# An attention and two-layer feed-forward kernel: its low parts and weight sums between GpSimd and VectorE, in a new order of the whole program

## The chip, the cores and the metric

One core of a Trainium2 chip runs the kernel. The metric is the device time of one execution in microseconds (us). PE is TensorE, DVE VectorE, ACT ScalarE, POOL GpSimd, and SP SyncE, which here issues all DMAs.

## The reference

```python
def _attn_ref(q, k, v):                      # (2, 8, 768, 64) each, float32
    k_sum = k.reshape(B, H, nb, 32, D).max(axis=3)
    v_sum = v.reshape(B, H, nb, 32, D).mean(axis=3)
    scores_l = scale * np.matmul(q, k.transpose(0, 1, 3, 2))
    mask_l = np.abs(pos[:, None] - pos[None, :]) < 16
    scores_s = scale * np.einsum('bhsd,bhnd->bhsn', q, k_sum) + np.log(32)
    a = softmax(concat([where(mask_l, scores_l, -1e9), scores_s]))
    return np.matmul(a, np.concatenate([v, v_sum], axis=2))

def _moe_ref(x, w_in, w_out):                # 1536 tokens, 512 -> 2048 -> 512
    h = x @ w_in
    return (h * np.clip(h + 3.0, 0.0, 6.0) / 6.0) @ w_out

def _moe2_ref(x, w_in, w_out):
    h = x @ w_in
    return (h / (1.0 + np.exp(-h))) @ w_out
```

The output is `_moe2_ref(_moe_ref(attention))`, with the heads side by side in the 512 columns.

## The kernel before

**Attention.** Each of the two batches has 12 windows of 64 queries. A window sees 96 neighbouring keys and 24 block maxima, so 120 columns for each pair of heads. `load` (L463) brings 256 rows of q, k or v: either by `load_pairs` (L456), two rows of 64 numbers in one piece of 512 bytes, followed by a reordering copy `by_parity` (L480, "par" in the order, one half on DVE and one on ACT); or by two DMAs in pieces of 256 bytes that land in the final order. `tr` transposes on PE (L500). `k_copy` and `k_max` (L504, L512) make the transposed keys and the block maxima. `keys u` (L586) gathers both into one tile for window u, and `scores n` (L596) multiplies them for the two windows 2n and 2n+1; it writes two banks, unit 2n for even heads and 2n+1 for odd ones. Then come `masked` (DVE, L616), `exps` (ACT, L634), `normal` (DVE or POOL, L654), `turn` (transposition on PE, L661), `turned` (its copy, L667) and `mix n` (product with the values, L672, PE rows L679). `load_v u` (L576) loads the values of window u, into one of four buffers while u is below 16, so that `load_v 4` to `load_v 7` wait for `mix 0` and `mix 1`. `mixed_hi` and `mixed_lo` (L697, L703) store the result in two parts: a rounded high part and, as the rest, a low part. `v_sums`, `v_add` and `v_rows` make the block means of v.

**Feed-forward.** Every operand is such a pair of high and low part, and each product is three matmuls (high-high, high-low, low-high). A weight half is fetched (`fetch h`, half 2f of w_in and 2f+1 of w_out), put together from its 16-bit pieces (`conv_top`, `conv_join`), and split into `conv_hi` (L443) and `conv_lo` (L448). A step is `hidden` (L711, PE, 12 matmuls in two parts), `act` (ACT), `gate` (DVE), `gate_hi` and `gate_lo` (L770, L774: the two parts of the gated values), and `project` (L803, PE rows L798 and L801). The first 24 steps go this way. The other 72 get their hidden values from seven products instead of eight (`prod` and `prodb`, PE rows L1025). These need sums and differences of weights (`ssum` L977, split by `s_hi`, `s_lo` L1006) and of tokens (`tsum`, split by `t_hi`, `t_lo` L927; `tsumb`, `t_hib`, `t_lob` L970), and DVE additions that join the products (`join` L1068, `joinb` L1056; rows L1072 and L1066).

**What sets the order.** One table, `ORDER`, names about 1,960 such operations in one sequence. The program records them in that sequence; each engine then runs its own in that order and waits by semaphores for the others. A star behind an entry puts it on DVE where the operation can go to two engines. `rouse` and `warm` are matmuls that compute nothing and keep PE running.

```python
def gate_lo(i):
    ...
    eng = nc.vector if STEPS[i][3] == WIDE or ("gate_lo", i) in ON_DVE else nc.gpsimd
```

All steps are WIDE (512 columns), so before the change every `gate_lo` is on DVE, as are all `ssum`, `s_lo`, `t_lo`, `t_lob` and `finish_lo` (L883, the low part of the first layer's output).

Of the kernel before, what the change touches and what calls it, by code (L numbers as in the profile page):

```python
# [111 lines left out]
load k 0 1, zero, table 0, rouse 0, warm 6, load k 0 2, par k 1 0, load k 0 0, par k 1 1, par k 2 1, grow 9,  # L112
par k 2 0, rouse 4, par k 0 1, tr k 0 1 0, k_copy 0 1 0*, tr k 0 1 1, load q 0 0, tr k 0 2 0, clear,
load k 1 0, par k 0 0, tr k 0 2 1, par q 0 1, k_copy 0 2 0*, rouse 5, tr k 0 0 0, fetch 0, k_max 0 2 0,
k_copy 0 0 0, par q 0 0, k_max 0 2 1, tr k 0 0 1, k_max 0 0 1, tr q 0 0 1, k_max 0 1 1, k_max 0 0 0,
k_max 0 1 0, k_copy 0 0 1, keys 1*, tr q 0 0 0, q_copy 0 0 0*, rouse 1, keys 2, k_copy 0 1 1, tr k 1 0 1,
tr k 1 0 0, k_max 1 0 1, q_copy 0 0 1, keys 3, scores 1, keys 0, k_copy 0 2 1, scores 0, keys 6, keys 4,
table 1, conv_top 0*, keys 5, rouse 3, masked 2, load q 0 1, load v 0 0, keys 7, tr q 0 1 0, exps 2, guard 2,
v_sums 0 0, q_copy 0 1 0, k_copy 1 0 1*, masked 0, exps 0, guard 0, masked 1, masked 3, inverse 2, exps 3,
tr q 0 1 1, normal 2, inverse 0, normal 0, guard 3, q_copy 0 1 1*, turn 2, turned 2, load q 0 2, load v 0 1,  # L120
load v 0 2, conv_join 0, exps 1, scores 2, rouse 2, turn 0, v_sums 0 1, grow 6, conv_hi 0*, inverse 3,
fetch 1, normal 3, turned 0*, v_add 0 0, masked 4, conv_lo 0, tr q 0 2 1, q_copy 0 2 1, k_max 1 0 0, guard 1,
inverse 1, tr q 0 2 0, exps 4, q_copy 0 2 0, v_add 0 1, v_sums 0 2, v_add 0 2, unstage, v_rows 0, scores 3,
conv_top 1*, normal 1, v_put 0 2*, turn 3, masked 6, load k 1 1, turn 1, masked 7, guard 4, v_put 0 0,
v_put 0 1, tr k 1 1 0, turned 3, v_put 0 3, conv_join 1, tr k 1 1 1, k_copy 1 1 0*, load k 1 2, exps 6,
k_copy 1 1 1, tr k 1 2 0, conv_hi 1*, masked 5, load_v 2, guard 6, inverse 6, inverse 4, load_v 0, exps 7,
k_max 1 2 0, k_max 1 1 0, keys 9, k_copy 1 0 0*, keys 11, keys 10, tr k 1 2 1, k_copy 1 2 1, scores 5,
load_v 3, load v 1 0, guard 7, normal 6, inverse 7, k_max 1 2 1, turn 6, normal 7*, mix 1, load_v 1,
k_copy 1 2 0, load q 1 0, normal 4, turn 7, masked 10, load_v 7, exps 5, masked 11, turned 1, load_v 6,
guard 5, turn 4, mix 0, turned 7*, keys 8, scores 4, turned 6*, exps 11, v_pair 1 0, guard 11, inverse 11,  # L130
inverse 5, conv_lo 1, k_max 1 1 1, load_v 4, v_sums 1 0, tr q 1 0 1, normal 5*, turned 4, normal 11, masked 8,
load_v 5, keys 12, exps 10, guard 10, tr q 1 0 0, inverse 10, q_copy 1 0 0, mixed_hi 1, turn 5, mixed_hi 0,
masked 9, turned 5, turn 11, mixed_lo 1, mix 3, normal 10, turn 10, q_copy 1 0 1*, load q 1 1, keys 13,
turned 11, mixed_hi 3*, mixed_lo 3, scores 6, fetch 2, turned 10, mixed_lo 0, keys 14, keys 15, mix 2,
scores 7, mixed_hi 2*, mixed_lo 2, tr q 1 1 1, exps 8, guard 8, exps 9, masked 14, inverse 8, tr q 1 1 0,
conv_top 2*, conv_join 2, guard 9, fetch 4, q_copy 1 1 0, hidden 0 0, q_copy 1 1 1, conv_top 4, hidden 0 1,
act 0, conv_hi 2*, inverse 9, normal 9*, normal 8, turn 8, conv_join 4, conv_hi 4*, masked 12, exps 14,
load v 1 1, conv_lo 2, load v 1 2, turned 8, exps 12, gate 0, gate_hi 0*, keys 17, guard 12, turn 9,
gate_lo 0, masked 13, hidden 1 0, hidden 1 1, turned 9, keys 16, scores 8, conv_lo 4, fetch 6, hidden 2 0,
conv_top 6, v_pair 1 1*, v_pair 1 2*, guard 14, load_v 8, exps 13, v_sums 1 1, conv_join 6, v_sums 1 2,  # L140
conv_hi 6, v_add 1 0, v_add 1 1, hidden 2 1, guard 13, inverse 12, normal 12*, v_add 1 2, act 1, masked 15,
inverse 13, normal 13*, load_v 9, grow 1, fetch 3, conv_top 3, conv_join 3, mix 4, gate 1, turn 12, turned 12,
v_rows 1, conv_hi 3*, act 2, v_put 1 0, masked 16, gate_hi 1, conv_lo 6, hidden 3 0, hidden 3 1, conv_lo 3,
gate 2, gate_hi 2*, mixed_hi 4, v_put 1 1, load_v 11, load_v 10, mix 5, gate_lo 1, mixed_lo 4, fetch 5,
conv_top 5, exps 15, mixed_hi 5, v_put 1 2, turn 13, fetch 8, conv_join 5, project 0 0, masked 17, conv_top 8,
conv_join 8, v_put 1 3, project 1 0, project 0 1, act 3, load_v 12, gate_lo 2, guard 15, conv_hi 8, keys 19,
project 1 1, conv_lo 8, fetch 7, conv_hi 5*, conv_lo 5, conv_top 7*, load_v 13, turned 13, mix 6, load q 1 2,
gate 3, inverse 14, inverse 15, mixed_hi 6*, conv_join 7, tr q 1 2 1, hidden 4 0, hidden 4 1, keys 18,
exps 17, guard 17, inverse 17, mixed_lo 6, mixed_lo 5, normal 14*, fetch 9, normal 15, conv_top 9*,
conv_join 9, exps 16, guard 16, conv_hi 7, q_copy 1 2 1, turn 15, turned 15, turn 14, turned 14*, normal 17,  # L150
turn 17, conv_lo 7, inverse 16, tr q 1 2 0, gate_hi 3, turned 17*, q_copy 1 2 0, project 2 0, normal 16*,
fetch 12, load_v 15, gate_lo 3, load_v 14, mix 7, scores 9, mixed_hi 7*, keys 20, mixed_lo 7, masked 19,
fetch 10, conv_top 10, project 3 0, turn 16, conv_join 10, act 4, conv_hi 10*, conv_lo 10*, masked 18, gate 4,
gate_hi 4*, conv_top 12, conv_join 12, exps 18, hidden 8 0, hidden 8 1, load_v 17, fetch 11, conv_hi 9,
conv_lo 9, hidden 10 0, hidden 10 1, act 8, gate 8, turned 16, act 10, project 3 1, conv_top 11, conv_join 11,
gate_hi 8*, conv_hi 11*, exps 19, guard 19, hidden 5 0, guard 18, hidden 5 1, gate_lo 4, project 4 0,
inverse 19, normal 19*, fetch 13, grow 0, conv_top 13, conv_lo 11, conv_join 13, act 5, load_v 16, turn 19,
gate 10, project 2 1, mix 8, mixed_hi 8, gate 5, fetch 14, conv_top 14*, inverse 18, conv_hi 13, gate_hi 5*,
gate_lo 5, keys 21*, turned 19*, hidden 11 0, hidden 11 1, project 5 0, act 11, normal 18, conv_hi 12*,
scores 10, conv_lo 13*, gate 11, load_v 19, fetch 18, turn 18, turned 18, conv_join 14, conv_hi 14, gate_lo 8,  # L160
load_v 18, keys 23*, masked 20, masked 21, conv_lo 12, conv_lo 14*, conv_top 18, conv_join 18, grow 5,
exps 20, project 4 1, fetch 15, hidden 6 0, conv_top 15*, keys 22, ssum 4 1, hidden 6 1, act 6, gate 6,
hidden 7 0, hidden 7 1, mix 9, gate_hi 6, gate_lo 6, tsum 0 1 1, exps 21, project 6 0, guard 21, act 7,
gate 7, hidden 12 0, hidden 12 1, load_v 21, guard 20, mixed_lo 8, inverse 20, normal 20*, conv_join 15,
conv_hi 15*, project 6 1, conv_lo 15, scores 11, fetch 16, inverse 21, act 12, normal 21*, project 5 1,
gate_hi 7, gate_lo 7, gate 12, gate_hi 12*, project 7 0, project 7 1, mixed_hi 9, turn 20, finish 0 0 0 0,
finish 0 0 0 2, masked 22, mixed_lo 9, finish 0 0 0 1, turn 21, turned 21, masked 23, exps 23, hidden 14 0,
turned 20*, hidden 14 1, act 14, conv_top 16*, gate_lo 12, project 8 0, hidden 13 0, load_v 20, hidden 13 1,
project 12 0, exps 22, guard 22, gate 14, inverse 22, normal 22, gate_hi 14, grow 2, gate_lo 14, mix 10,
load_v 22, turn 22, turned 22, guard 23, inverse 23, normal 23, project 8 1, project 12 1, turn 23,  # L170
project 14 0, grow 3, conv_join 16, grow 8, mixed_hi 10*, mixed_lo 10, ssum 4 2, turned 23, ssum 4 3, act 13,
# [1103 lines left out]
```

## Time and profile before

| | |
|---|---|
| median of 3 executions | 585.9 us (585.74 to 586.0) |
| the profiled execution | 585.98 us |
| its span, first to last instruction | 584.1 us |
| PE busy | 566.9 us, 97% of the span, granted clock 1.00 |
| DVE busy | 462.3 us, 79% |
| ACT busy | 269.6 us, 46% |
| POOL busy | 95.8 us, 16% |

The profiled execution took 1.9 us more than its span, which is the start and the end around it. A busy share is a mean: the first 50 us are attention alone, and from then on attention, feed-forward steps and weights overlap. Instructions that are pipelined overlap in the rows by some 0.1 us, and matmuls by up to 0.17 us, because their ends are modelled; so this text takes the time of a piece of work from its start to the start of the next.

### The profile page before, as it was taken

Reading aid. Unit: us, or ns where it says so; the run is one execution under the profiler, and the core shown is the slowest. Engines: PE = TensorE matmul, PEld = TensorE weight load, DVE = VectorE, ACT = ScalarE, POOL = GpSimd, SP = SyncE. Lnnn points to the kernel's source line nnn. Section 1 sums busy time; section 2 is a strip of 40 time slices with the busy share of each in tenths; the row PEclk is TensorE's granted clock in tenths of the full one; section 3 lists DMA queues with packets and bytes.
Section 4 is the critical chain, followed back from the end, with each engine's and each line's share of the span. In section 5 each row is a group of like instructions: output and inputs, shape, how many; then the busy total and the mean of one; then the engine's idle time right before and its main releaser. Section 6 shows DMA issues by size and latency. Waiting matters only on the chain.

```text
span 584.1 us, 9467 instructions
## 1 busy us (share of the span) xinstructions
PE 566.9 (97%) x3536; PEld 476.7 (82%) x3536; DVE 462.3 (79%) x1012; ACT 269.6 (46%) x626; POOL 95.8 (16%) x111
## 2 busy tenths in 40 slices
PE   6778999999999999999999999999999999999997
PEld 6667788888888788888888888888888898888886
DVE  4899888874776999998999999585877686757764
ACT  4798865542313345541646565545534234424220
POOL 1756252101010012121100202000100000111000
PEclk9999999999999999999999999999999999999999
DMA  9999982323010112333220110223122211210013
GB/s 239 258 191 261 214 202 87 100 64 98 0 38 0 51 57 73 109 89 119 80 71 3 37 37 30 79 77 125 50 73 83 98 37 36 73 66 8 1 71 146
DMA packets 69054, 51.57 MB, mean 88 GB/s; under 512 B 36368, under 2 KB 63504, under 8 KB 69008
## 3 DMA queue, kind: packets, MB, share of 16 engines
q1 hardware_dynamic: 69008, 50.97, 33.2%
q8 instruction: 28, 0.46, 0.3%
...
## 4 chain that ended last, share of the span: by engine, by line
PE 88%; DVE 5%; DMA 3%; ACT 2%; issue 1%; SPq 0%; POOL 0%; DVEq 0%
PE bank L1025 29%; PE bank L801 22%; PE bank L798 20%; PE bank L721 11%; PE bank L679 2%; PE bank L665 1%; DMA stage<-in_v_dram 1%; PE bank L608 1%; DMA early_units<-in_v_dram 1%; ACT early_units L637 1%; DVE kmax L514 1%; DMA cst<-in_consts_dram 1%; PE bank L500 1%; DVE w L928 0%; DVE bits L435 0%
## 5 line engine op out<-in xcount | busy, mean ns | idle before, releaser
L801 PE MATMUL bank<-w,g 128*128 128x512 f32 (+1 forms) x477 | 111.7, 385 | 0.0
L798 PE MATMUL bank<-g,w 128*128 128x512 f32 x444 | 108.7, 391 | 0.4 <-DVE g L778 0.4
L801 PEld LDWEIGHTS bank<-w,g 128*128 128x128 f32 x477 | 88.2, 188 | 17.7
L450 POOL TENSOR_TENSOR w<-bits,w 128x512 fp32r<-128x512 f32 x34 | 47.9, 1411 | 304.0 <-ACT w L446 213.5
L798 PEld LDWEIGHTS bank<-g,w 128*128 128x128 f32 x444 | 82.5, 188 | 17.7 <-DVE g L778 0.8
L1025 PE MATMUL bank<-w,x 128*128 128x512 f32 (+1 forms) x360 | 73.9, 348 | 0.5 <-DVE w L971 0.5
L1025 PEld LDWEIGHTS bank<-w,x 128*128 128x128 f32 x360 | 59.4, 189 | 10.0 <-DVE w L971 0.8
L1025 PE MATMUL bank<-x,w 128*128 128x512 f32 (+1 forms) x240 | 49.6, 348 | 0.0
L426 ACT CAST top<-words 128x512 f16<-128x512 bf16 x51 | 39.7, 778 | 19.9 <-DVE bits L435 11.0
L721 PE MATMUL bank<-x,w 128*128 128x512 f32 x192 | 47.7, 396 | 0.0
L435 DVE SCALAR_TENSOR_TENSOR bits<-words,top 128x512 uint32<-128x512 uint32 x47 | 35.6, 756 | 14.0 <-ACT top L426 11.8
L1025 PEld LDWEIGHTS bank<-x,w 128*128 128x128 f32 x240 | 39.1, 189 | 5.5
L721 PEld LDWEIGHTS bank<-x,w 128*128 128x128 f32 x192 | 35.3, 188 | 7.8 <-issue 0.4
L778 DVE TENSOR_TENSOR g<-values,g 128x512 fp32r<-128x512 f32 x46 | 32.6, 712 | 7.4 <-ACT g L772 7.0
L752 ACT ACTIVATE values<-values 128x512 f32<-128x512 f32 x35 | 22.0, 628 | 29.3 <-DVE values L1066 17.0
L798 PE MATMUL bank<-w,w 128*128 128x512 f32 x132 | 33.6, 392 | 0.0
L752 ACT ACTIVATE r<-r 128x512 f32<-128x512 f32 x27 | 17.0, 629 | 28.9 <-DVE r L1072 20.0
L1072 DVE TENSOR_TENSOR values<-bank,values 128x512 f32<-128x512 f32 x39 | 26.5, 687 | 3.1 <-PE bank L1025 2.6
L798 PEld LDWEIGHTS bank<-w,w 128*128 128x128 f32 x132 | 24.5, 188 | 5.1 <-issue 0.2
L450 POOL TENSOR_TENSOR w<-cst,w 128x512 fp32r<-128x512 f32 x10 | 14.2, 1418 | 87.8 <-DVE w L446 60.6
L1025 PE MATMUL bank<-w,w 128*128 128x512 f32 (+1 forms) x144 | 28.1, 337 | 0.0
L772 ACT CAST g<-values 128x512 fp32r<-128x512 f32 x33 | 20.4, 621 | 16.7 <-PE bank L801 6.5
(192 smaller groups left out, 984.8 us busy)
## 6 DMA issues: line engine op xcount, KB each, us to landing
...
```

The costliest lines, as they stand in the source:

```text
L426: copier("conv_top", h)(out=top[:, 1], in_=src[:, 2])
L435: nc.vector.scalar_tensor_tensor(out=bitss.take(h, bit_users(h)), in0=rest, scalar=13, in1=tops.use(h).bitcast(U32), op0=ALU.logical_shift ...
L450: eng.tensor_tensor(out=w_half(h, 1), in0=bitss.use(h).bitcast(F32), in1=w_half(h, 0).bitcast(F32), op=ALU.subtract,)
L679: nc.tensor.matmul(ps[D * e : D * e + D, o : o + QW], v[:NSLOT, h * D : (h + 1) * D], own(pTs, 2 * n + e)[:NSLOT, hp * P + QW * w : hp * P ...
L721: nc.tensor.matmul(ps[:, :n], w[:, a, kk * P : (kk + 1) * P], x[:, o // SUB : (o + n) // SUB, b, kk, :], start=(m == 0), stop=(m == last),)
L752: nc.scalar.activation(out=r, in_=ps, **kind)
L772: copier("gate_hi", i)(out=g[:, 0, cols], in_=value(i)[:, cols])
L778: eng.tensor_tensor(out=g[:, 1, cols], in0=r[:, cols], in1=g[:, 0, cols].bitcast(F32), op=ALU.subtract)
L798: nc.tensor.matmul(ps[:, o : o + n], lhs, g[:, b, shift : shift + n], **flags)
L801: nc.tensor.matmul(ps[:, : len(cols)], g[:, a, rows], rhs, **flags)
L1025: nc.tensor.matmul(ps, lhs(a, kk), rhs(b, kk), start=(i == 0), stop=(i == 5))
L1072: nc.vector.tensor_tensor(out=out, in0=banks.use(("prod", p, k)), in1=r, op=ALU.add)
```

## The change

Five things change.

- `gate_lo`, `ssum`, `s_lo`, `t_lo`, `t_lob` and `finish_lo` may now go to POOL. 20 of 96 `gate_lo`, 17 of 48 `ssum`, 18 of 48 `s_lo`, 11 of 16 `t_lo`, 3 of 8 `t_lob` and 4 of 10 `finish_lo` do. The other way, 14 of 44 `conv_lo`, 7 of 21 pairs of `keys` copies and 5 of 14 `normal` move from POOL to DVE.
- The first q block is loaded in two DMAs by parity, without `load_pairs` and `by_parity`.
- The first `scores` reads the keys and maxima where they lie, in 32 matmuls for 16, and `keys 0` and `keys 1` go.
- The three `v_sums` of a batch add up in one bank, and `v_add` is one copy for a copy and two additions.
- The `ORDER` table is new except for its last 463 entries, which stand in the same sequence, some on another engine; there are 12 `rouse` for 6.

```diff
+    def adder(*op):
+        return (nc.vector if op in ON_DVE else nc.gpsimd).tensor_tensor
...
-        if b == 0 and (what == "k" or T == 0):
+        if b == 0 and what == "k":
             load_pairs(parts.take((what, b, T), 2), src, b, T)
...
+        if done == 0:
+            banks.take(("v", b), 1)
+        ps = banks.see(("v", b))
...
-                    start=(r == 0),
-                    stop=(r == 1 - b),
+                    start=(done == 0 and r == 0),
+                    stop=(done == 2 and r == 1 - b),
...
+    def v_add(b):
+        nc.vector.tensor_copy(out=vsum, in_=banks.use(("v", b))[:, :P])
...
+        if n < DIRECT:
+            near = [key_rows(b)[:, :, (t + w) * QW : (t + w) * QW + LOC] for w in range(2)]
+            pieces = [(0, near), (LOC, [kmax[b]] * 2)]
+        else:
+            pieces = [(0, [own(kws, 2 * n + w) for w in range(2)])]
...
-        eng = nc.vector if STEPS[i][3] == WIDE or ("gate_lo", i) in ON_DVE else nc.gpsimd
+        eng = nc.vector if ("gate_lo", i) in ON_DVE else nc.gpsimd
...
-        nc.vector.tensor_tensor(
+        adder("t_lo", layer, a, n)(
...
-gate_hi 82*, gate_lo 77, fetch 60, project 77 0, gate_hi 78, gate_lo 78, project 77 1, gate_hi 79,
+gate_hi 82*, gate_lo 77*, fetch 60, project 77 0, gate_hi 78, gate_lo 78*, project 77 1, gate_hi 79,
```

**SP, the loads that stand ahead of the values of windows 4 and 5.** Before, from the load of the second v block (`stage` with in_v) on; `early_w` with in_k or in_q are the 256-byte loads, `words` are weights, `early_units` and `early_r` with in_v are `load_v`, and `early_w` with in_v is `load v 1 0`, the first v block of batch 1:

```order
L458 DMA stage_84<-in_v_dram 128x8x128
L458 DMA stage_80<-in_v_dram 128x8x128
L418 DMA words_70<-in_moe_w_out_dram 128x2047
L473 DMA early_w_88<-in_k_dram 128x8x64 x4
L581 DMA early_units<-in_v_dram 96x8x64
L581 DMA early_r_97<-in_v_dram 80x8x64
L581 DMA early_units<-in_v_dram 96x8x64
L458 DMA early_w_88<-in_v_dram 128x8x128
L581 DMA early_r_97<-in_v_dram 96x8x64
L473 DMA early_w_88<-in_q_dram 128x8x64 x2
L581 DMA early_units<-in_v_dram 96x8x64 x2
L581 DMA early_r_97<-in_v_dram 96x8x64 x2
```

The same stretch now, to the same last row:

```order
L478 DMA early_w_88<-in_k_dram 128x8x64 x2
L478 DMA early_w_88<-in_q_dram 128x8x64 x2
L588 DMA early_units<-in_v_dram 96x8x64
L421 DMA words_69<-in_moe_w_in_dram 128x4x511
L588 DMA early_r_97<-in_v_dram 96x8x64
L423 DMA words_70<-in_moe_w_out_dram 128x2047
L588 DMA early_units<-in_v_dram 96x8x64
L478 DMA early_w_88<-in_k_dram 128x8x64 x2
L588 DMA early_r_97<-in_v_dram 80x8x64
L478 DMA early_w_88<-in_q_dram 128x8x64 x2
L588 DMA early_units<-in_v_dram 96x8x64 x2
L588 DMA early_r_97<-in_v_dram 96x8x64 x2
```

`load v 1 0` has left this stretch; it now stands two weight halves behind its end. Every other load up to the last row stands ahead of it before and now, among themselves in another order.

**PE, the first feed-forward step.** The names are `scores` (L608), `tr` of the next q block (L500), `hidden` (L721, 12 matmuls a step) and `turn` (L665). Before, from the end of `scores 7` on:

```order
L608 MATMUL bank_72<-early_units,early_w_89 64x120 x2
L500 MATMUL bank_73<-cst,early_w_88 128x128 x4
L500 MATMUL bank_74<-cst,early_w_88 128x128 x4
L721 MATMUL bank_79<-x_0_64,w_87 128x512 x12
L665 MATMUL bank_77<-cst,early_w_95 120x128 x4
L665 MATMUL bank_74<-cst,early_w_95 120x128 x4
L721 MATMUL bank_73<-x_0_64,w_386 128x512 x12
```

Now:

```order
L680 MATMUL bank_72<-cst,early_units 120x128 x4
L680 MATMUL bank_74<-cst,early_w_95 120x128 x4
L736 MATMUL bank_78<-x_0_64,w_86 128x512 x12
L736 MATMUL bank_79<-x_0_64,w_87 128x512 x12
L623 MATMUL bank_75<-early_units,early_w_89 64x120 x2
```

`turn 9`, which stood between the first two steps, now stands ahead of both, together with one more turn, and the two steps follow each other. `scores 7`, `v_sums 1 0`, `turn 11` and both `tr q 1 1` (the two L500 rows) have gone from ahead of the first step to behind the second.

**POOL, in the middle of the program** (the first weight sums of the seven-product scheme). Before, only `conv_lo` (L450) and the last `normal` (L657) stand there:

```order
L450 TENSOR_TENSOR w_1265<-bits_67,w_1265 128x512
L657 TENSOR_TENSOR early_w_95<-early_w_95,stat_103 128x480
L657 TENSOR_TENSOR early_w_95<-early_w_95,stat_100 128x480
L450 TENSOR_TENSOR w_1594<-cst,w_1594 128x512
L450 TENSOR_TENSOR w_1594<-bits_68,w_1594 128x512
```

Now `gate_lo` (L793), `ssum` (L1009), `t_lo` (L943), `t_lob` (L986) and `s_lo` (L1023) stand among the `conv_lo` (L455):

```order
L793 TENSOR_TENSOR g_92<-values,g_92 128x512
L1009 TENSOR_TENSOR words_70<-bits_68 128x256
L1009 TENSOR_TENSOR words_70<-bits_67,bits_68 128x256
L1009 TENSOR_TENSOR words_70<-words_70,bits_67 128x256
L1009 TENSOR_TENSOR words_70<-bits_67,words_70 128x256
L793 TENSOR_TENSOR g_1719<-values,g_1719 128x512
L455 TENSOR_TENSOR w_1544<-bits_68,w_1544 128x512
L943 TENSOR_TENSOR w_491<-values,w_491 128x512
L986 TENSOR_TENSOR x_late<-r_1720,x_late 128x512
L1023 TENSOR_TENSOR x_1_65<-words_70,x_1_65 128x256 x2
```

Eleven low parts and sums that were DVE's are POOL's here, with one `conv_lo` among them.

## Rows read from the trace of the kernel before

**Rows 1.** Page: busy time, share of the span and instructions of each engine.

```profile
PE 566.9 (97%) x3536; PEld 476.7 (82%) x3536; DVE 462.3 (79%) x1012; ACT 269.6 (46%) x626; POOL 95.8 (16%) x111
```

**Rows 2.** Stage: us, busy time (instructions) of PE, PEld, DVE, ACT, POOL; clock, DMA share, GB/s.

```profile
30.00:45.00 15.00, 11.49 (x190) 9.37 (x188) 13.54 (x74) 13.92 (x57) 9.73 (x15) 1.00 1.17 192
```

**Rows 3.** Waits of PE from 51 to 575 us: total, times, longest.

```profile
PE bank L1025 <- DVE w L971: 0.5, 1, 0.5
PE bank L798 <- DVE g L778: 0.4, 1, 0.4
```

**Rows 4.** PE in order of time, 40 to 62 us: start, length, instructions, [idle before].

```profile
40.11 0.69 PE L679 MATMUL bank<-early_g,early_r 120*64 120x64 f32 x16 [0.54 <-DMA early_r<-in_v_dram]
...
47.65 1.15 PE L679 MATMUL bank<-early_g,early_r 120*64 120x64 f32 x32
48.73 1.05 PE L608 MATMUL bank<-early_units,early_w 64*64 64x120 f32 x32
49.85 1.09 PE L500 MATMUL bank<-cst,early_w 128*128 128x128 f32 x8
50.70 3.00 PE L721 MATMUL bank<-x,w 128*128 128x512 f32 x12
53.54 0.60 PE L665 MATMUL bank<-cst,early_w 128*120 128x128 f32 x4
55.35 0.62 PE L665 MATMUL bank<-cst,early_w 128*120 128x128 f32 x4 [1.21 <-DVE early_w L657]
55.73 3.01 PE L721 MATMUL bank<-x,w 128*128 128x512 f32 x12
...
59.65 1.67 PE L721 MATMUL bank<-x,w 128*128 128x512 f32 x6
61.25 0.71 PE L545 MATMUL bank<-early_w,cst 128*32 128x128 f32 x16
```

**Rows 5.** DVE in order of time, 48 to 54 us.

```profile
48.85 0.69 DVE L701 CAST x<-bank 128x512 fp32r<-128x512 f32 x1 [0.57 <-PE bank L679]
49.57 0.69 DVE L705 TENSOR_TENSOR x<-bank,x 128x512 fp32r<-128x512 f32 x1
...
53.45 1.75 DVE L657 TENSOR_TENSOR early_w<-early_w,stat 128x480 f32<-128x480 f32 x1
```

**Rows 6.** SP's issues in order of time, and the landing of the load issued at 31.78.

```profile
30.74 0.67 SPq L581 DMA_DIRECT2D early_units<-in_v_dram  x1
31.78 0.66 SPq L458 DMA_DIRECT2D early_w<-in_v_dram  x1
...
41.16 1.60 SPq L581 DMA_DIRECT2D early_r<-in_v_dram  x2
...
DMA to landing us min/median/max: 7.3/7.3/7.3
```

**Rows 7.** The landing of the load issued at 30.74.

```profile
DMA to landing us min/median/max: 6.0/6.0/6.0
```

**Rows 8.** ACT, released by the landings of the k block 0 and the first q block.

```profile
8.91 0.62 ACT L486 COPY stage<-stage 128x512 f32<-128x512 f32 x1 [1.18 <-DMA stage<-in_k_dram]
10.78 0.62 ACT L486 COPY stage<-stage 128x512 f32<-128x512 f32 x1 [1.25 <-DMA stage<-in_q_dram]
```

**Rows 9.** The landing of the next load's second half, in pieces of 256 bytes.

```profile
L473 SPq DMA_DIRECT2D early_w<-in_k_dram x1: 1736/1736/1736, 7.0 to 7.0; - x1
...
DMA to landing us min/median/max: 6.1/6.1/6.1
```

**Rows 10.** By line: one instruction in ns, min/median/max, first and last start.

```profile
L778 DVE TENSOR_TENSOR g<-values,g x46: 676/686/1776, 68.8 to 565.0; 128x512 fp32r<-128x512 f32 x46
L1072 DVE TENSOR_TENSOR values<-bank,values x39: 680/685/693, 228.7 to 557.7; 128x512 f32<-128x512 f32 x39
L450 POOL TENSOR_TENSOR w<-bits,w x34: 1274/1302/1823, 25.0 to 538.5; 128x512 fp32r<-128x512 f32 x34
```

**Rows 11.** Busy time by stage, columns as in rows 2, in the seven-product part.

```profile
200.00:225.00 25.00, 24.50 (x130) 20.84 (x129) 24.13 (x46) 8.81 (x17) 2.48 (x2) 1.00 0.16 52
```

More of the change, by code (lines that the diff above doesn't have):

```diff
@@ L111 @@
 ORDER = """
[L112 to L171, printed above, removed]
@@ new lines @@
+normal 9, mix 3, mixed_hi 3*, mix 2, scores 6, mixed_lo 0, k_copy 1 1 1, turn 10, mixed_hi 2, mixed_lo 3,
+mixed_lo 2, fetch 2, conv_top 2, exps 11, fetch 4, keys 17*, conv_join 2, conv_hi 2, turn 9, masked 13,
+hidden 0 0, hidden 0 1, k_copy 1 2 0, conv_top 4, conv_lo 2*, turned 10, keys 15, hidden 1 0, hidden 1 1,
+guard 11, keys 14, scores 7, masked 12, conv_join 4, load v 1 0, inverse 11, act 0, gate 0, v_pair 1 0*,
+grow 1, turned 9, v_sums 1 0, normal 11, turned 8*, turn 11, load q 1 1, conv_hi 4, conv_lo 4, exps 13,
@@ new lines @@
+conv_hi 10, guard 14, v_put 1 3*, conv_lo 10*, v_put 1 2, hidden 5 0, act 4, gate_hi 3, gate 4, load q 1 2,
+tr q 1 2 1, fetch 7, inverse 14, hidden 5 1, exps 16, project 2 1, gate_lo 3, mixed_lo 4, mixed_lo 5,
+normal 14*, conv_top 7*, conv_join 7, act 5, conv_hi 7, fetch 9, gate 5, q_copy 1 2 1*, keys 18*, guard 16,
+conv_lo 7*, inverse 17, turn 15, turn 14, conv_top 9*, load_v 13, load_v 12, normal 17*, load_v 15, gate_hi 5,
+mix 6, turned 14, tr q 1 2 0, grow 0, inverse 16, normal 16, conv_join 9, project 3 0, project 3 1, fetch 11,
@@ new lines @@
+project 6 0, gate_lo 7*, hidden 15 0, hidden 15 1, act 15, fetch 18, hidden 13 1, turn 19, exps 20,
+conv_lo 15, project 7 0, guard 20, masked 21, project 6 1, act 13, turned 19, exps 21, load_v 18, grow 5,
+load_v 19, project 7 1, mix 9, load_v 21, inverse 20, normal 20*, keys 23*, gate 13, gate_hi 8*,
+finish 0 0 0 0, keys 22, conv_top 19*, conv_join 19, scores 11, grow 2, guard 21, inverse 21, gate 15,
+finish 0 0 0 1, fetch 16, conv_top 18, conv_hi 19*, turn 20, turned 20, normal 21*, turn 21, turned 21,
@@ new lines @@
+finish 0 0 0 3, gate_lo 8, project 8 0, masked 23, hidden 14 0, hidden 14 1, masked 22, exps 22, exps 23,
+act 14, guard 22, load_v 20, project 9 0, finish 0 0 0 2, guard 23, mix 10, hidden 12 0, conv_lo 19,
+inverse 23, normal 23*, inverse 22, project 8 1, project 9 1, normal 22*, gate_hi 15, hidden 12 1, gate 14,
+gate_hi 10, turn 22, gate_lo 10*, mixed_hi 10, mixed_hi 9, mixed_lo 9, tsum 0 3 0, act 12, load_v 22,
+turned 22, gate 12, turn 23, conv_join 18, gate_lo 15, project 10 0, hidden 11 0, gate_hi 14, mixed_lo 10,
```

373 lines of the change are left out of this document (206 added, 167 removed).

## Prediction

> **What bounds the kernel now.** I read the page first. PE is busy for 97% of the span, DVE for 79%, POOL for 16% [rows 1]. A change that moves work between DVE and POOL can therefore only gain what PE loses by waiting, and the question is where that is. From 51 to 575 us PE waited three times for more than a moment: the two shortest [rows 3], and the one of 1.21 us at 55.35, where `turn 9` waits for `normal 9` [rows 4]. Together these are 2.1 us. The rest of the idle time lies ahead of 51 us: in 30 to 45 us PE is busy for 11.5 of 15 us, while DVE has 13.5, ACT 13.9, and the DMA share is above 1 [rows 2]. So the head of the program is held by loads and by two engines at once, and ends where the first feed-forward step starts, at 50.70 [rows 4]. From there on PE has filler work for nearly every moment.
>
> What holds that first step is a chain that the rows show link by link. `mix 0` waits for a load of values until 40.11. Its end frees the buffers for the values of windows 4 and 5, which SP issues from 41.16 [rows 6]. `mix 2`, which reads them, starts at 47.65 [rows 4]; `mixed_hi 2` starts at 48.85 and `mixed_lo 2` at 49.57 [rows 5]; PE fills in `scores 7` and two transpositions, and the step starts at 50.70. The chain's first link is the SP queue.
>
> **The head: loads.** All loads that stood ahead of `mix 0`'s last one, and of those of windows 4 and 5, stand ahead of them after the change too, except `load v 1 0`. Its price: it was issued at 31.78 and landed 7.3 later, at 39.1; the load before it was issued at 30.74 and landed 6.0 later, at 36.7 [rows 6, 7]. The queue thus gave it 2.4 us, which the chain no longer waits for. Against this, the first q block now comes in pieces of 256 bytes. In pieces of 512 it took from 8.91 to 10.78, 1.87 us [rows 8]; the k block behind it, of the same size in pieces of 256, ended at 7.0 + 6.1 = 13.1, so it took 2.3 [rows 9]. That is 0.4 more. The Trainium skill's page "DMA: Bandwidth & Descriptors", section "Specifications", asks for at least 512 bytes in a transfer for the full rate and so speaks against this edit; the trace agrees in the sign, by a quarter and not more. If the chain keeps its length of 10.6 us, the first step starts at 50.70 - 2.4 + 0.4 = 48.7.
>
> This isn't a gain of 2 us, because less has been done by then. `scores 7` (48.73 to 49.85, 1.1), two transpositions (to 50.70, 0.85), one `turn` (55.35 to 55.73, 0.4) and half of the 0.7 that two `v_sums` take now come later; two turns (0.8) come earlier [rows 4]. Net 1.9 us of PE's work is still to do, so the start that changes nothing is 50.70 - 1.9 = 48.8. The term is **-0.1**. Its bounds: if the q block costs nothing more, -0.5; if the chain isn't led by the queue but by DVE, which the next paragraph prices, +3.
>
> **The head: the other engines.** `keys 0`, `keys 1`, two reordering copies and two `v_add` on DVE and ACT go; DVE takes five `normal`, several `keys` and two `conv_lo` or so of POOL's. I count about 1.2 us more of DVE work ahead of `mixed_lo 2` than before, at 0.6 to 0.7 for an instruction of 512 columns [rows 10]. DVE had 1.5 us of 15 free [rows 2], some 4 us over 45, so it is covered if DVE's waits fall well, and costs 1.2 if not. I take nothing. The twice 16 matmuls of the first `scores` for 1.05 us [rows 4] and the six more `rouse` lie where PE has nothing else to do; if not, they cost 1 us. One copy for three `v_add`s is off the chain as well.
>
> **The wait at 55.35.** `normal 9` stood on DVE behind a POOL instruction and took 1.75 us [rows 5]; `turn 9` behind the first step waited for it. Now `turn 9` stands ahead of the first step and its `normal` is POOL's, early. The wait goes: **-1.2**. What could be late instead is the second step, which now follows the first at once; its low part of weights is DVE's, after `mixed_lo 2`, and has the 2.84 us of the first step for two casts and a subtraction. I take nothing for it, and 0.5 as its bound.
>
> **Fewer changes of kind.** From the first step on PE alternated between runs of feed-forward and attention 19 times, now 17. A run of 12 matmuls took 2.84 (50.70 to 53.54), one of six 1.60 (59.65 to 61.25), 0.18 more than half of that [rows 4]. Two runs fewer: **-0.4**, and nothing as the other bound.
>
> **The middle.** These two waits [rows 3] are for a `t_lo` and a `gate_lo` on a DVE that is busy for 24.1 of 25 us there [rows 11]. DVE hands over 38 instructions of 512 columns at 0.69, 26 us, and 35 of 256; it takes back 14 `conv_lo` and, on balance, some 15 others, at most 20 us. It has more room, and I let both waits go: **-0.9**.
>
> What POOL's side costs: a low part takes 1.30 there against 0.69, and each holds up the other engine. The DVE row of `gate_lo`, two operands in SBUF, goes from 686 up to 1776 ns; the row that reads a bank never exceeds 693; POOL's own goes from 1302 up to 1823 [rows 10]. The Trainium skill's page "SBUF — State Buffer", section "Who interferes with whom", calls this an exclusive lock of a shared port, by which the later of the two waits for the whole instruction of the other; it speaks against every move to POOL. By the rows a move costs the chain behind it at most 1.82 - 0.69 = 1.1 plus one blocked instruction of 1.1. The chain from a product to the `project` that reads it is a join, `act`, `gate` and `gate_hi` at about 0.7 each, and the low part: 4.1 to 4.6 us with POOL. In the new order at least 24 matmuls lie between, 33 where POOL makes the low part; at 2.84 / 12 = 0.24 these are 5.7 and 7.8 us. In the old order the shortest lead was some 17, 4 us, and left no wait at its place [rows 3]. I take nothing for new waits; the bound is 15 places of 0.3, +4.5.
>
> **Sum.** 585.98 - 0.1 - 1.2 - 0.4 - 0.9 = 583.4, made against the profiled execution, which is 0.1 above the median of 585.9. I forecast **583.4**, 0.4% faster. About 0.2% (1.2 us) is what a measurement of this kernel can tell from no change.
>
> **Rivals.**
> - *The head comes late by what is saved.* DVE or ACT lead the chain, and the 1.2 us of extra DVE work and its waits push the first step to 51 or so: 583.4 + 2.3 = 585.7. For it: DVE 13.5 and ACT 13.9 of 15 [rows 2]. Against: the rows at 40.11 and 47.65 show loads at the head of the chain. It's the case in which the change does nothing.
> - *One queue wait holds all of SP* (slower). `load q 1 0` needs a buffer that a transposition frees which now stands on PE behind `turn 6`, and that waits for DVE's `normal 6`. SP is in order, so the four loads of values stand behind it. If `normal 6` is 4.5 us late, the first step starts at 53.2: 583.4 + 4.5 = 587.9. From a start at 51.3 on it's no gain at all, and each us is a us. For it: the loads at 41.16 were issued only when `mix 0` had ended [rows 6], so SP does stand still in this stretch; against: nothing shows `normal 6` that late.
> - *POOL as the new wait* (slower by the same mark): the lock above, at 15 of the 73 new places for 0.3 us: 587.9. It decides from 2.6 us of new waits on. For it: POOL's instructions are 1.3 to 1.8 long; against: the leads.
> - *The head gains more*: loads run 2 us ahead of the old queue because fewer of them wait for a buffer, and the first step starts at 46.7: 581.4. DVE has too little room for more.
>
> **How the numbers follow.** Forecast 0.48, head late 0.2, queue wait 0.1, POOL 0.1, larger gain 0.12. The forecast's own range, with the bounds of the q block, the second step, the alternations and 1 us of new waits, is 582.2 to 585.0; I count 0.46 of its 0.48 as faster by over 0.2%, with the larger gain 0.58. The late head is within 0.2%, with the rest of the forecast 0.22. The two others make 0.2 slower. The range for 8 times in 10 reaches from 581.2 to 587.2.
>
> **What would show it.** The first step's start (48.7; no gain from 51.3 on), the end of `mix 0` and the last landing ahead of `mix 2`; no wait at `turn 9`; 17 runs; PE's waits from 51 to 575 us, with their releasers: none by POOL over 0.3 us if I'm right. DVE's busy time should fall by 10 to 30 us and POOL's rise by 30 to 60 with no effect on the time. The prediction is wrong if PE waits for POOL at many places, or if the first step starts at 51 or later.

## The result: 0.7% slower

The changed kernel took 589.9 us in the median of 4 runs (589.59 to 590.79) beside 585.85 us for the kernel before, a ratio of 1.0067 (95% interval 1.0056 to 1.0079). A second series gave 1.0064 (1.0049 to 1.0078). The forecast was 583.4 us, its range 581.2 to 587.2: wrong in sign, and outside the range.

The page of the profiled execution (589.95 us, span 588.2): busy time, and the busy tenths of 40 slices for DVE, POOL and PE's clock.

```profile
PE 572.0 (97%) x3592; PEld 481.1 (82%) x3592; DVE 459.8 (78%) x971; ACT 262.1 (45%) x617; POOL 151.9 (26%) x151
...
DVE  4789989766869898888989999647677687657764
...
POOL 1136313421030743222223474423310000111000
PEclk9989999999999999999999999999999999999999
```

POOL took 56 us more than in [rows 1], DVE only 2.5 less. PE's waits from 51 to 575 us, as in [rows 3] (total, times, longest):

```profile
PE bank L1040 <- DVE acc L862: 2.2, 2, 1.9
PE bank L1040 <- DVE values L1087: 0.8, 1, 0.8
PE bank L816 <- DVE r L1087: 0.6, 1, 0.6
PE bank L680 <- DVE early_w L672: 0.5, 1, 0.5
PE bank L813 <- DVE g L793: 0.2, 1, 0.2
```

These are 4.3 us, all for DVE, none for POOL; [rows 3] had 0.9 beside the wait at 55.35. Matmuls' ends are modelled, so a part of a gap is missing there. By the spacing of PE's starts, less the usual spacing of the same shape, the waits from 53 to 578 us are 5.6 us now. Before they are 1.65 us beside the one at 55.35, which is 1.4 by this count. So the middle of the program has 4.0 us more of waits. Of the 5.6, 0.7 lie at 130 us and 0.4 at 266; the rest is between 314 and 363, where the first layer goes over into the second.

PE around the end of the head, as in [rows 4] (start, length, instructions, [idle before]):

```profile
33.38 0.75 PE L623 MATMUL bank<-early_w,early_w 64*64 64x120 f32 x16 [1.71 <-ACT early_w L534]
...
40.09 0.65 PE L680 MATMUL bank<-cst,early_units 128*120 128x128 f32 x4 [1.09 <-POOL early_units L672]
40.58 0.60 PE L505 MATMUL bank<-cst,early_w 128*128 128x128 f32 x4
41.11 1.15 PE L694 MATMUL bank<-early_g,early_r 120*64 120x64 f32 x32
43.02 0.62 PE L680 MATMUL bank<-cst,early_w 128*120 128x128 f32 x4 [0.76 <-ACT stat L663]
...
50.09 5.72 PE L736 MATMUL bank<-x,w 128*128 128x512 f32 x24
55.73 1.05 PE L623 MATMUL bank<-early_units,early_w 64*64 64x120 f32 x32
```

The first step starts at 50.09; the forecast was 48.7, the start that changes nothing 48.8. Two steps now follow at once (24 matmuls), and `turn 9` waits no more. And `mix 0` (41.11) stands behind `turn 7`, which waits for POOL's `normal 7`, not for a load. From 28 to 51 us the view of PE's waits lists ACT three times (2.9 us) and POOL once (1.1), and no load. The stage of 30 to 45 us, columns as in [rows 2]:

```profile
30.00:45.00 15.00, 10.96 (x170) 9.37 (x169) 13.00 (x74) 13.25 (x58) 6.03 (x9) 0.89 1.09 188
```

PE's granted clock is 0.89 where it was 1.00: after a wait of 1.71 us, PE worked from 33.9 to 37.3 at the lower of its two levels (1.2 GHz).

DVE and POOL ahead of the longest wait, which ends at 328.38:

```profile
311.96 1.67 DVE L969 TENSOR_TENSOR values<-acc 128x512 f32<-128x512 f32 x1
313.55 0.68 DVE L793 TENSOR_TENSOR g<-values,g 128x512 fp32r<-128x512 f32 x1
...
316.71 1.79 DVE L969 TENSOR_TENSOR values<-acc,r 128x512 f32<-128x512 f32 x1
...
324.24 1.19 DVE L986 TENSOR_TENSOR w<-values,w 128x512 fp32r<-128x512 f32 x1
325.35 1.77 DVE L793 TENSOR_TENSOR w<-r,w 128x512 fp32r<-128x512 f32 x1
327.05 0.68 DVE L440 SCALAR_TENSOR_TENSOR bits<-words,top 128x512 uint32<-128x512 uint32 x1
327.65 1.87 DVE L862 SCALAR_TENSOR_TENSOR acc<-bank,acc 128x512 f32<-128x512 f32 x3
```

```profile
311.78 1.30 POOL L900 TENSOR_TENSOR x<-acc,x 128x512 fp32r<-128x512 f32 x1
316.34 1.60 POOL L986 TENSOR_TENSOR x<-r,x 128x512 fp32r<-128x512 f32 x1 [3.26 <-ACT x L980]
323.56 1.31 POOL L793 TENSOR_TENSOR g<-r,g 128x512 fp32r<-128x512 f32 x1 [5.62 <-ACT g L787]
324.84 1.73 POOL L986 TENSOR_TENSOR w<-values,w 128x512 fp32r<-128x512 f32 x1
```

From 312 to 330 us DVE doesn't pause. Four of its instructions take 1.2 to 1.8 us for 0.68, each beside one of POOL's. `finish` (L862), which PE waits for, reads a bank and isn't held up (676 to 692 ns for each of its 24 rows); it is late by what stands ahead of it.

To compare kernels I call *hold-up* what an instruction takes beyond the tenth percentile of those of its line and form, from 0.1 us on, and add it up. DVE's hold-ups rose from 22.0 to 39.4 us, from 300 to 350 us from 1.1 to 8.1. There DVE was busy for 48.70 us of 50 before and for 47.44 now: the exchange of work bought it 1.3 us. Over the whole program DVE's time without the hold-ups fell from 440.3 to 420.4 us, so the move did take 20 us of work off DVE; 17 of them came back as hold-ups.

### The profile page after: what moved, and what is told of

Read it like the earlier page. It is cut to its first block, busy times and chain, and to the rows that moved or that the text cites. A ratio compares the mean times of both kernels' runs of the same rounds, so it can differ in the third digit from the quotient of the medians.

```text
span 588.2 us, 9556 instructions
## 1 busy us (share of the span) xinstructions
PE 572.0 (97%) x3592; PEld 481.1 (82%) x3592; DVE 459.8 (78%) x971; ACT 262.1 (45%) x617; POOL 151.9 (26%) x151
## 3 DMA queue, kind: packets, MB, share of 16 engines
HBM read 47.81 MB, written 3.15 MB: 87 GB/s over the span
## 4 chain that ended last, share of the span: by engine, by line
PE 83%; DVE 10%; DMA 2%; ACT 1%; SPq 1%; issue 1%; POOL 1%; DVEq 0%
PE bank L1040 26%; PE bank L816 21%; PE bank L813 18%; PE bank L736 11%; PE bank L694 2%; PE bank L680 2%; PE bank L623 1%; DMA early_w<-in_q_dram 1%; DVE g L793 1%; DVE acc L862 1%; DMA early_w<-in_k_dram 1%; SPq L478 1%; PE bank L505 1%; DVE values L931 1%; DVE values L969 1%
## 5 line engine op out<-in xcount | busy, mean ns | idle before, releaser
L813 PE MATMUL bank<-g,w 128*128 128x512 f32 x408 | 100.5, 392 | 0.3 <-DVE g L793 0.2
L816 PE MATMUL bank<-w,g 128*128 128x512 f32 (+1 forms) x393 | 92.8, 386 | 0.6 <-DVE r L1087 0.6
L813 PEld LDWEIGHTS bank<-g,w 128*128 128x128 f32 x408 | 75.6, 188 | 16.5 <-DVE g L793 1.1
L816 PEld LDWEIGHTS bank<-w,g 128*128 128x128 f32 x393 | 72.0, 188 | 15.6 <-DVE r L1087 1.1
L455 POOL TENSOR_TENSOR w<-bits,w 128x512 fp32r<-128x512 f32 x20 | 28.0, 1401 | 97.2 <-ACT w L451 75.9
L816 PE MATMUL bank<-w,w 128*128 128x512 f32 (+1 forms) x195 | 47.3, 386 | 0.0
L813 PE MATMUL bank<-w,w 128*128 128x512 f32 x168 | 42.9, 394 | 0.0
L816 PEld LDWEIGHTS bank<-w,w 128*128 128x128 f32 x195 | 36.2, 188 | 7.3
L431 ACT CAST top<-words 128x512 f16<-128x512 bf16 x40 | 31.3, 782 | 23.7 <-DVE bits L440 11.1
L813 PEld LDWEIGHTS bank<-w,w 128*128 128x128 f32 x168 | 31.0, 188 | 6.6 <-issue 0.2
L793 DVE TENSOR_TENSOR g<-values,g 128x512 fp32r<-128x512 f32 x36 | 27.2, 762 | 8.1 <-ACT g L787 7.8
L455 POOL TENSOR_TENSOR w<-cst,w 128x512 fp32r<-128x512 f32 x10 | 14.3, 1429 | 59.9 <-DVE w L451 34.9
L1040 PE MATMUL bank<-w,w 128*128 128x256 f32 (+1 forms) x144 | 28.4, 337 | 0.0
```

Of the source, the lines that this page charges most:

```text
L431: copier("conv_top", h)(out=top[:, 1], in_=src[:, 2])
L455: eng.tensor_tensor(out=w_half(h, 1), in0=bitss.use(h).bitcast(F32), in1=w_half(h, 0).bitcast(F32), op=ALU.subtract,)
L793: eng.tensor_tensor(out=g[:, 1, cols], in0=r[:, cols], in1=g[:, 0, cols].bitcast(F32), op=ALU.subtract)
L813: nc.tensor.matmul(ps[:, o : o + n], lhs, g[:, b, shift : shift + n], **flags)
L816: nc.tensor.matmul(ps[:, : len(cols)], g[:, a, rows], rhs, **flags)
L1040: nc.tensor.matmul(ps, lhs(a, kk), rhs(b, kk), start=(i == 0), stop=(i == 5))
```

## The experiments

"Before" is 586.1 to 586.2 us beside the runs below. Theory A: POOL's long low parts and DVE's hold-ups make the new waits. B: the order does. C: the head does.

**Low parts moved back, all or some.** `e1`, `e4`, `e9` star 73, 24 or 3 entries; `e2` gives them their new places in the old order. The moves the other way stay as they are in either kernel: in e1 DVE also has the `conv_lo`, `keys` and `normal` that the change gave it, in e2 POOL keeps all of its own.

```diff
-t_lob 1 1, gate_lo 42, ... t_lob 1 3,
+t_lob 1 1*, gate_lo 42*, ... t_lob 1 3*,
```

> The changed kernel with all 73 low parts and weight sums that it gives to POOL back on DVE; the order, the head and the value sums stay as changed. Theory A (POOL's twice as long low parts, and the locks between POOL and DVE, make the new waits of PE): the 4.0 us of new waits between 53 and 578 us go, 589.9 - 4.0 = 585.9 us, between 585.2 and 586.6, no wait of PE over 1 us after 53, and DVE's time above its shortest durations falls from 39 to about 22 us. Theory B (the new order, in which PE asks for results earlier, makes them): 589 to 590, with the waits at the same places. Theory C (the head, 1.2 us later than forecast with a lower clock, is the loss): 589 to 590 with the first feed-forward step near 50.

> The kernel before, in its own order and with its own head, where the same 73 low parts and weight sums are POOL's and all others of these kinds are DVE's. Theory A: 3 to 6 us of new waits behind the long low parts, 588.9 to 592 us. Theory B: 585.3 to 586.5, as before, since the order has its leads. Theory C: 585.3 to 586.5, since the head is the old one.

> The changed kernel with only the 24 low parts and sums that POOL made between 299 and 375 us, around the change of layer, back on DVE; the 49 others stay on POOL. Theory A in its narrow form (the loss is made at the change of layer, where DVE is busy without a pause): 3 to 4 us come back, 586.0 to 587.0. In its wide form (each place costs a little): 24 of 73 places, 1.3 us, 588.6. Theory B or C: 589 to 590.

> The changed kernel with three of POOL's low parts back on DVE: t_lob 1 1, gate_lo 42 and t_lob 1 3, which POOL made from 316 to 327 us while DVE's instructions beside them took 1.2 to 1.8 us in place of 0.68. Theory A in its narrow form (there the locks cost DVE more than the work they take off it): the wait of 2.1 us at 328.4 goes, 1.5 to 2.2 us less, 587.7 to 588.4. Theory D, read from the four runs so far (DVE is the bound there by its own work, and each low part more makes it later): the wait grows by 0.5 to 2 us, 590.4 to 592.

Measured: e1 605.3 us (ratio 1.0329, 1.0313 to 1.0344), e2 605.7 (1.0335, 1.0318 to 1.0353), e4 593.8 (1.0134, 1.0119 to 1.0149), e9 589.3 (1.0045, 1.0030 to 1.0060). No theory had expected e1 and e4: A was too simple. DVE's hold-ups fell to 13.5 us in e1, but its time without them rose from 420.4 to 455.1, and the kernel was 15.4 us slower than the changed one. PE's waits in e4 show how:

```profile
PE bank L1042 <- DVE w L945: 4.5, 2, 4.3
PE bank L1042 <- DVE x L1025: 0.9, 1, 0.9
PE bank L1042 <- DVE x L988: 0.8, 1, 0.8
```

L945 is `t_lo`: DVE, in order and busy, makes it 4.3 us too late. So the new order does need POOL there. Laid against the changed kernel matmul by matmul, e4 is ahead by 1.1 us more behind the wait at 328, where `t_lob 1 1`, `gate_lo 42` and `t_lob 1 3` had moved. It loses 4.6 us at the `t_lo` and 1.6 more right behind it, where PE works at the lower clock. e9 moves those three alone: the wait of 1.9 us goes, a wait of 0.8 for `t_lob` comes, and of 1.6 us gained by then 0.4 is left at the end. e2 shows the other side: the old order with POOL's low parts loses 19.6 us, 3.5 of it in one wait for a `conv_lo` behind them on POOL, which is busy for 181.1 us there. Places and order only work together, so neither B nor A can be read from moves. What is needed is a run that keeps both.

**The same order and places, POOL's instructions shorter.** `e7` makes them short and leaves work out; `e16` halves those of 512 columns, `e19` quarters them, `e17` and `e18` halve `conv_lo` in the kernel before and in e16.

```diff
-        return (nc.vector if op in ON_DVE else nc.gpsimd).tensor_tensor
+        if op in ON_DVE:
+            return nc.vector.tensor_tensor
+
+        def halved(out, in0, in1, op):
+            wide = len(out.shape) == 2 and out.shape[1] == WIDE
+            parts = [slice(0, WIDE // 2), slice(WIDE // 2, WIDE)] if wide else []
...
+            for k in parts or [slice(None)]:
+                nc.gpsimd.tensor_tensor(out=out[:, k], in0=in0[:, k], in1=in1[:, k], op=op)
```

> The changed kernel in which 47 of POOL's 73 low parts and sums, those after 200 us except three t_lob, four finish_lo and the first s_lo of the second layer, work on 64 of 512 or 256 columns only, so that POOL and the locks are short; the rest of those low parts is left out and holds older values. Order, places and DVE's instructions stay. Theory A (POOL's long low parts and their locks make the waits at 266, 314 to 328, 353 and 363 us, 4.9 us together): 2.5 to 4.5 us come back, 585.4 to 587.4, and DVE's time above its shortest durations falls by over 10 us. Theory B (the order asks DVE for more than it can make there, whatever POOL does): at most 1 us comes back, 588.9 to 590.

> The changed kernel with POOL's low parts of 512 columns each made by two instructions of 256, in the same places; conv_lo and all others stay. POOL's work grows by some 0.2 us for each. Theory A1 (DVE loses time since it is held up for the whole of one long instruction of POOL): a hold-up is at most 0.75 us in place of 1.1, DVE's time above its shortest durations falls from 39 to 25 to 30 us, the wait of 2.1 us at 328 shrinks below 1.2, 588.0 to 589.2 us. Theory A2 (what counts is POOL's time in all): DVE is held up twice, 589.9 to 591.

> The kernel before with POOL's conv_lo made by two instructions of 256 columns. Theory A1: normal 9 on DVE is held up for 0.5 us less, the wait of 1.21 us at 55.35 falls to about 0.7, 0.4 to 0.8 us below before. Theory A2: within 0.4 us of before, or slower.

> The changed kernel with both, POOL's low parts and its conv_lo in two instructions of 256 columns. Theory A1: a little better than with the low parts alone, 587.6 to 589.0 us. Theory A2: 590 to 592.

> The changed kernel with POOL's low parts of 512 columns made by four instructions of 128. If shorter hold-ups of DVE go on paying: below the 586.4 of two halves, 585.0 to 586.2. If POOL's fixed time for each instruction eats it up: 586.4 to 588.

Measured: e7 584.7 us (0.9976, 0.9966 to 0.9987), e16 586.4 (1.0007, 0.9997 to 1.0016), e17 586.2 (0.9999, 0.9988 to 1.0010), e18 587.0 (1.0018, 1.0007 to 1.0029), e19 588.3 (1.0033, 1.0020 to 1.0047). In e7, with order, places and DVE's instructions as in the changed kernel, 5.2 us go: 1.1 in the head and 4.1 behind it, 3.4 of these in PE's waits, which by the spacing of starts fall from 5.6 to 2.2 us. But e7 also gives POOL less to do, so it can't tell the hold-ups from POOL's work; e16 can. e7's starts lie ahead of the changed kernel's by 1.1 us from 42 on (the head's clock, below), by 1.6 after 266, 3.4 after 328, 4.4 after 353 and 5.2 after 363 us: each wait named above, one after the other. What is left of PE's waits, first in e7, then in e16, where the output is whole:

```profile
PE bank L1099 <- DVE acc L921: 1.1, 1, 1.1
PE bank L740 <- DVE early_w L732: 0.5, 1, 0.5
PE bank L1099 <- DVE values L1146: 0.2, 1, 0.2
```

```profile
PE bank L1052 <- DVE acc L874: 0.6, 2, 0.4
PE bank L693 <- DVE early_w L685: 0.5, 1, 0.5
PE bank L825 <- DVE g L805: 0.4, 2, 0.2
PE bank L1052 <- POOL w L411: 0.4, 1, 0.4
```

e16 gives POOL more to do (164.3 us) and is 3.5 to 3.8 us faster than the changed kernel in its two series, more than A1 had expected. Laid against it matmul by matmul, 1.1 us lie in the head, where the clock stays up, and 2.4 behind it, 2.2 of these in PE's waits, which fall from 5.6 to 3.4 us. So A1 holds for 2.2 of the 4.0 us of new waits: what hurts is that DVE is held up for a whole long instruction. The other 1.8 are left in e16. DVE's hold-ups there, 32.9 us for 22.0 before, would fit them, but no run shows their cause. DVE and POOL in e16, the same place as above:

```profile
323.24 0.68 DVE L998 TENSOR_TENSOR w<-values,w 128x512 fp32r<-128x512 f32 x1
323.84 0.68 DVE L805 TENSOR_TENSOR w<-r,w 128x512 fp32r<-128x512 f32 x1
324.44 0.68 DVE L453 SCALAR_TENSOR_TENSOR bits<-words,top 128x512 uint32<-128x512 uint32 x1
325.04 1.88 DVE L874 SCALAR_TENSOR_TENSOR acc<-bank,acc 128x512 f32<-128x512 f32 x3
```

```profile
322.57 3.15 POOL L411 TENSOR_TENSOR g<-r,g 128x256 fp32r<-128x256 f32 x2 [5.02 <-ACT g L800]
325.68 1.44 POOL L411 TENSOR_TENSOR w<-values,w 128x256 fp32r<-128x256 f32 x2
```

Now POOL is held up (3.15 us for two halves, 2.43 of them for the second), and DVE runs through at 0.68. From DVE's row at 311.96 us of the changed kernel (310.87 in e16) to this `finish`, its hold-ups fall from 3.7 us (four of 0.5 to 1.1) to 2.2 (four of 0.55). Over the whole program they fell less than expected, so the gain seems to be in where they fall and how long each is; no run separates these. Quarters go too far: hold-ups of DVE 27.9, but POOL's four take 0.59 each in the mean, and PE now waits for it:

```profile
PE bank L1052 <- POOL w L411: 1.8, 2, 1.4
PE bank L1052 <- DVE acc L874: 1.0, 1, 1.0
```

e17 is a miss: `turn 9`'s wait fell to 0.7 as A1 says, and the time didn't move; PE waited longer for a load of k in the head (2.9 us in place of 1.3). e18 is no better than e16, and slower in its median.

**The head.** `e3` makes the three small edits in the old order. `e6` puts `rouse` ahead of the scores at 33.4, `e20` does so in e16. `e15` is the changed kernel again.

```diff
-turned 1, fetch 0, exps 6, masked 7, q_copy 0 2 1, keys 11*, scores 4,
+turned 1, fetch 0, exps 6, masked 7, q_copy 0 2 1, keys 11*, rouse 20, rouse 21, rouse 22, rouse 23, scores 4,
```

> The kernel before in its own order with the three small edits alone: the first scores row by row without two keys, the first q block by two DMAs of 256-byte pieces, value sums in one bank; low parts on DVE. Theories A and B: within 0.6 us of before, 585.3 to 586.5, as the head's end is set elsewhere. Theory C: the head loses 1 to 3 us, 587 to 589, with the first feed-forward step at 52 or later in place of 50.7.

> The changed kernel with eight dummy matmuls of 128 columns on PE (four rouse of two, at about 0.16 us each) ahead of the scores for which PE waited 1.71 us at 33.4. Theory C1 (that wait lowers the clock, and the slow matmuls up to 37.3 make the head 1.2 us late): the granted clock of 30 to 45 us rises from 0.89 to about 1.0, the first feed-forward step starts near 48.9, 588.7 us. Theory C2 (POOL, ACT and DVE lead the head, PE's clock is covered): the clock rises, and the time stays within 0.4 us of 589.9.

> The changed kernel as it is. If its 1.25 us late head (granted clock 0.89 in 30 to 45 us, first feed-forward step at 50.09) belongs to the order, the times lie together at 589.9 to 590.4. If the lower clock comes and goes with the same program, as two runs with this head and a clock of 1.00 suggest, the times spread over two groups some 1.2 us apart, 588.6 to 588.9 and 589.8 to 590.1.

> The changed kernel with POOL's low parts in halves and with the eight dummy matmuls ahead of the scores at 33.4. If the two are independent: 0.5 us below the 586.4 of the halves alone, 585.6 to 586.2. If the head is led by POOL and ACT and the clock stays up without them: 586.2 to 586.8.

Measured: e3 587.1 us (1.0017, 1.0007 to 1.0026), e6 589.3 (1.0053, 1.0034 to 1.0071), e15 590.1 (1.0064, 1.0049 to 1.0078), e20 586.3 (1.0001, 0.9993 to 1.0010). e3's first step starts at 51.90, 1.2 us later than before [rows 4]: in the old order the small edits cost 1.0 us, about what C says for them; which of the three wasn't tried apart. In e6 the clock stayed at 1.00 in 30 to 45 us and the step started at 49.35, but behind the wait at 328 the matmuls were slow (clock 0.66 in 328 to 333 us), and the gain of 0.6 is within the intervals. Two of e6's five executions had a mean granted clock of 1.00 and took 589.9 and 590.2 us, so a clock that stays up is no sure gain of 1.1 us; why not is open. e20 gained 0.1 on e16 by the same edit, where the clock had stayed up without it. e15 fits neither way that I had put. In its profile the head had the full clock and the step started at 49.50 (48.85 in e4, 48.97 in e16, 49.00 in e7, all with the same head), and the total was the same. The lost time had moved, to right behind the other long wait (stage 328 to 332 us, then PE there):

```profile
328.00:332.00 4.00, 4.00 (x15) 3.22 (x15) 2.00 (x4) 2.13 (x4) 1.61 (x2) 0.59 0.42 131
```

```profile
327.79 0.98 PE L1040 MATMUL bank<-x,x 128*128 128x256 f32 x6 [1.95 <-DVE acc L862]
328.61 2.69 PE L813 MATMUL bank<-g,w 128*128 128x512 f32 x6
331.09 2.01 PE L813 MATMUL bank<-w,w 128*128 128x512 f32 x6
```

The matmuls start 0.43 us apart there, for 0.23 usually. All nine runs of the changed kernel in the two series had a mean granted clock of 0.994 to 0.997.

**The old order, with one step of the prediction each.** `e11` moves the one load that the prediction priced, with the `v_pair` and `v_sums` that use it, `e14` moves it one place further; `e10` makes `normal 9` early on DVE, `e12` is e10 and e11, `e8` moves `turn 9`.

```diff
-load v 1 0, guard 7, ... load_v 5, keys 12,
+guard 7, ... load_v 5, load v 1 0, keys 12,
```

```diff
-conv_top 2*, conv_join 2, guard 9, ... conv_hi 2*, inverse 9, normal 9*,
+guard 9, inverse 9, normal 9*, conv_top 2*, conv_join 2, ... conv_hi 2*,
```

> The kernel before with the one move of loads that my prediction priced: load v 1 0 behind load_v 5 on the queue, v_pair 1 0 and v_sums 1 0 with it. If the queue leads the chain through mix 0 and mix 2, as I predicted, the first feed-forward step starts 2.4 us earlier, near 48.3, with 0.35 us of PE's work moved behind it: 1.5 to 2.1 us below before. If DVE, ACT or POOL lead it, loads land early for nothing: the step starts at 50.2 or later, and the time is within 0.5 us of before.

> The kernel before with load v 1 0 behind load q 1 1, one place later than in the run that moved it behind load_v 5; v_pair 1 0 and v_sums 1 0 stand as there. In that run the loads of values for mix 2 landed 2.9 us earlier, no wait for them was left, and the first feed-forward step started at 50.19, behind a new wait of 0.88 us for load q 1 1. If that wait was all that held it, the step starts near 49.3 and the time is 1.3 to 1.7 us below before. If DVE or ACT hold the step then, it starts at 50 or later: 0.4 to 0.8 us below before, as in that run.

> The kernel before with one edit: guard 9, inverse 9 and normal 9 stand ahead of conv_top 2, so that DVE makes normal 9 before the conversions in place of behind them and beside POOL's conv_lo 2, which held it up to 1.75 us. If the wait of 1.21 us at 55.35 was caused by that alone, it goes and DVE gains the 1.05 us of the lock: 1.2 us below before (1.0 to 1.6). If the conversions, now 0.7 us later, hold the feed-forward steps behind: within 0.4 us of before.

> Both edits of the kernel before together. If they are independent, the sum of the two: by my prediction's chain 3.0 us below before, without it 1.2 us below.

> The kernel before with one entry moved: turn 9 behind hidden 1 1 on PE, so that the second feed-forward step doesn't stand behind the wait of 1.21 us at 55.35. If that wait was its own and nothing else was late: 585.9 - 1.2 = 584.7 us, between 584.2 and 585.1, at one change of kind less for PE. If the low part of weights for the second step or its values are late in its place: 585.5 to 586.2.

Measured: e11 585.4 us (0.9990, 0.9981 to 0.9999), e14 587.95 (1.0025, 1.0014 to 1.0037), e10 586.3 (1.0006, 0.9998 to 1.0015), e12 585.9 (1.0001, 0.9989 to 1.0013), e8 589.0 (1.0042, 1.0026 to 1.0059). In e11 the last load ahead of `mix 2` landed at 44.18, before at 47.12, and PE waited for no load of values. Yet the step started only 0.5 us earlier:

```profile
48.24 0.33 PE L503 MATMUL bank<-cst,early_w 128*128 128x128 f32 x1
49.45 0.98 PE L503 MATMUL bank<-cst,early_w 128*128 128x128 f32 x7 [0.88 <-DMA early_w<-in_q_dram]
50.19 3.01 PE L724 MATMUL bank<-x,w 128*128 128x512 f32 x12
```

e14 took away that new wait for q too, and its step started at 51.13, behind waits of 1.81 us for a load of k and 1.03 for DVE. This is one of e14's slowest executions (589.17; they go from 585.76 to 589.35). Of the 3.2 us by which it ends behind the kernel before, only 0.4 stand at the first step; the rest is a longer wait at `turn 9` (1.97 us) and slow matmuls behind it. In both runs a load out of the way opened another gap, so loads don't lead the head by themselves. e10 took the wait at `turn 9` away: 1.6 us ahead of the kernel before there, it was level by 61.3 us, through waits of 0.56 us for POOL's `conv_lo 2` inside the second step and 0.50 for a copy on DVE. e12 adds nothing to e11. e8's edit was badly chosen: windows 9 and 13 share a buffer, and `turn 9` now stands behind `masked 13`, which fills it anew. So it waited 2.43 us for that and took window 13's numbers for its own; its time says nothing about the wait at 55.35.

e11 is the one version with the whole output below both kernels, by 0.1% against before, and its interval ends at 0.9999: at the edge of what can be told. The best whole form of the change, e16 or e20, equals the kernel before.

## Why the prediction was wrong

Against the profiled execution: 585.98 before; the head +1.3 (50.09 less 48.8) where I had -0.1; `turn 9` -1.4, by the spacing of starts, where I had -1.2; the middle +4.0 where I had -0.9; together 589.9, measured 589.95. The runs of feed-forward fell from 19 to 17 as I counted; that this is worth 0.4 us can't be seen in this and was tested by no run.

- **"I take nothing for new waits" failed**: they were 5.6 us, in seven places, and passed the bound of 4.5. Since 1.65 us of old waits went, the middle is +4.0 for -0.9, 4.9 of the 6.5 us. I had compared a chain of 4.1 to 4.6 us, with one hold-up in it, with a lead of 24 matmuls. That holds for an engine which is free when the chain reaches it. DVE stood in an unbroken queue of 18 us there, and every hold-up ahead adds to all that follow: 3.7 us in four. e16 against the changed kernel shows it for 2.2 us of the waits, where nothing but the length of POOL's instructions differs. The rule that I had set aside is the Trainium skill's exclusive lock, in "SBUF — State Buffer", section "Who interferes with whom". The trace agrees: DVE's row at 325.35 took 1.77 us beside 1.73 of POOL's, and 0.68 in e16.
- **"It has more room, and I let both waits go" (-0.9)** came out at its two places: DVE was busy for 36.75 us from 185 to 225 us, before for 38.02, and PE waits there no more. It failed as a statement on the whole middle: from 300 to 350 us 7.0 us more of hold-ups used up nearly all that had left DVE.
- **The head's -0.1.** The start of 48.7 was close where the clock stayed up (48.85 to 49.50 in e4, e16, e7 and e15), but by luck, for the reason was wrong. I had the SP queue lead the chain. The row at 47.65, which I took for a load at its head, names none; in the changed kernel PE's waits from 28 to 51 us are for ACT and POOL; and e11 shows the old queue worth 0.5 us of the 2.4. The other 1.1 us of the loss are, in this profile, the lower clock behind a long wait, which I had not priced; in e15 the same loss came behind the wait at 328 instead.
- **The forecast's own range** of 582.2 to 585.0 doesn't follow from the bounds that I named for it: they give 583.0 (0.4 less by the q block) to 585.3 (0.5 more by the second step, 0.4 by the alternations and 1 us of waits).
- **Right:** the wait at 55.35 went at its price, and nothing was late for the second step. In the old order that price isn't to be had alone: e10 took the wait away and gained nothing. That the q block costs 0.4 more wasn't tested by itself.
- **Of the rivals** "POOL as the new wait" came, at a chance of 0.1. It was right in the mechanism, but 15 places of 0.3 us were 7 places of 0.3 to 2.1. My sign for it, a wait of PE for POOL, would have missed it: the view names DVE every time, for the hold-ups that POOL causes are in the length of DVE's own rows.

That halves of POOL's instructions gain because DVE gets in between them is shown at the place above; that it is so at every other wait is argued from e7 and e16's totals.
